# One store in twenty is cut into 119 and 9 partitions

## The chip, the cores and the metric

The kernel runs on one core of one Trainium2 chip. The metric is the device time of one execution in microseconds. The core has five engines that run their own instruction streams: TensorE (PE), VectorE (DVE), ScalarE (ACT), GpSimd (POOL) and SyncE (SP). SP computes nothing here; it issues DMAs, which sixteen DMA engines carry out.

## The reference

It is the forward and the backward pass of decode attention: one query row for each of 2 x 32 heads, against 8192 keys and values of width 128, all in bf16.

```python
B, H, Sq, Sk, D = 2, 32, 1, 8192, 128

def _fwd_reference(q, k, v):
    scale = q.shape[-1] ** -0.5
    scores = jnp.einsum("bhqd,bhkd->bhqk", q, k) * scale
    p = _softmax(scores, axis=-1)
    return jnp.einsum("bhqk,bhkd->bhqd", p, v)

def reference(q, k, v, grad_out):
    _out, _vjp = jax.vjp(_fwd_reference, q, k, v)
    _grads = _vjp(grad_out)
    return (_out, *_grads)
```

K and V of a head are 2 MB each. So 64 heads read 268 MB, and the gradients dK and dV write as much again. The output and dQ are small.

## The kernel before, in words

A head's K and V are loaded whole, as tiles `kt` and `vt` of 128 partitions x 64 rows x 128 (`load`, L103). Partition p holds 64 consecutive rows, which are 16 KB of contiguous memory. Five such pairs exist (`UNITS = 5`).

TensorE transposes the rows eight at a time against an identity (`transposes`, L112). ScalarE, and for two steps in sixteen VectorE, copies the transposes out of PSUM (L119, L117), and TensorE multiplies them with the query and with the output's gradient (`products`, L135). Softmax and its gradient then need a few small operations per head (L159 to L227). The weighted sums for the output and dQ are matmuls over the untransposed rows (`weighted_rows`, L240).

dV and dK are outer products of a weight per row with one row of `grad_out` or `q`. VectorE writes them into the buffers from which the rows came (`outer`, L270): dV into `vt`, and dK into `kt`, four pieces of 16 rows each. After the fourth piece `store` (L278) writes the whole 2 MB tile to memory; w = 0 is dV and w = 1 is dK. For the last head alone it stores halves of 1 MB.

The order is written out by hand (`manual_schedule`). In iteration h the program works on head h (transposes, products, softmax) and finishes head p = h - 1 (weights, outer products, stores). At its end it issues the load of head h + 3 into the pair of buffers that head h - 2 has left:

```python
if j == 7:
    if x and UNITS <= h + 3 < BH:
        load(h + 3)
```

All loads and stores of K, V, dK and dV are issued by SP in this order, so in the middle of the run each iteration gives SP a dV store, a dK store, a K load and a V load. A load waits until the store out of its buffer has landed. What stands behind a waiting DMA in SP's order waits with it. The two small inputs and the two small outputs go through ACT's DMA queue.

Of the kernel before, what the change touches and what calls it, by code (L numbers as in the profile page):

```python
# [15 lines left out]
HC = CH // 2  # L16
QG = 4
OG = 4
UNITS = 5


@with_exitstack
def kernel(
# [11 lines left out]
    nc = tc.nc  # L35
    B, H, Sq, D = q.shape
    Sk = k.shape[2]
    P = nc.NUM_PARTITIONS
# [3 lines left out]
    assert NT * P == Sk and NT == 4 * CH and BH <= P and BH % QG == 0  # L42
    assert BH % OG == 0 and OG * 8 == 32
    NS = 2 * NT // CH
# [9 lines left out]

    pick = const.tile([P, 4, 2, OG], F32)
    idv = ident_f[:].rearrange("p (g w k j) -> p g j w k", g=4, w=2, k=OG)
    nc.vector.tensor_copy(out=pick[:], in_=idv[:, 0])
    for g in range(1, 4):
# [6 lines left out]

    kvp = ctx.enter_context(tc.tile_pool(name="kv", bufs=UNITS))
    evp = ctx.enter_context(tc.tile_pool(name="ev", bufs=5))
# [8 lines left out]
    dk_v = out_2.rearrange("b h (p n) d -> (b h) p n d", n=NT)  # L76
    dv_v = out_3.rearrange("b h (p n) d -> (b h) p n d", n=NT)
# [8 lines left out]
    wz = [  # L86
        [const.tile([P, NT // 4, 32], BF16, name=f"wz{w}{k}") for k in range(OG)]
        for w in range(2)
# [5 lines left out]
    heads = [Head() for _ in range(BH)]  # L94

    def load(h):
        x = heads[h]
        x.kv = [
            kvp.tile([P, NT, D], BF16, name="kt", tag="kt"),
            kvp.tile([P, NT, D], BF16, name="vt", tag="vt"),  # L100
        ]
        for dst, src in zip(x.kv, (k_v, v_v)):
            nc.sync.dma_start(out=dst[:], in_=src[h])  # L103
# [79 lines left out]
    def to_weights(h, w, src):  # L183
        k = h % OG
        nc.vector.tensor_copy(  # L185
            out=wz[w][k][:, :, 16 * w + 4 * k : 16 * w + 4 * k + 4],
            in_=src[:].rearrange("p (m j) -> p m j", j=4),
        )
# [44 lines left out]
    def weighted_rows(h, w, chunks):  # L233


        rows, k = heads[h].kv[1 - w], h % OG
        for c in chunks:
# [37 lines left out]
        )  # L275

    def store(h, w, a=0, b=NT):
        nc.sync.dma_start(out=(dv_v, dk_v)[w][h][:, a:b, :], in_=heads[h].kv[1 - w][:, a:b, :])  # L278

    def outer_and_store(h, w, i):  # L280

        outer(h, w, i)
        if h == BH - 1:
            if i % 2:
                store(h, w, (i - 1) * CH, (i + 1) * CH)
        elif i == NT // CH - 1:
            store(h, w)
# [13 lines left out]
    with tc.manual_schedule():  # L301
        for h in range(min(UNITS, BH)):
            load(h)
        for h in range(BH + 1):
# [4 lines left out]
            for j in range(NS):  # L309
# [31 lines left out]
# [3 lines that stand above are left out]
# [38 lines left out]
```

## Time and profile before

| what | value |
|---|---|
| three runs | 1332.49, 1332.11, 1324.77 us; median 1332.11 |
| the profiled execution, its own time | 1328.14 us |
| its span, first to last instruction | 1326.3 us |
| PE, ACT, DVE busy | 84%, 68%, 67% of the span |
| DMA queue of SP | 536.89 MB, 98.2% of sixteen engines' span |
| data read and written, over the span | 405 GB/s |
| K loads and V loads, issue to landing (median) | 25.4 us, 30.2 us |
| dV stores and dK stores, issue to landing (median) | 34.8 us, 39.5 us |

The DMA share is the mean over the sixteen engines of the time in which a packet was under way. A packet here is one partition's 16 KB. Issue to landing counts from SP's instruction until all parts of the transfer have arrived, time in the DMA engines' own queues included. The profile does not number the DMA engines. It does keep, for each DMA, the times of the sixteen steps by which its semaphore rises.

### The profile page before, as it was taken

How to read it: one execution, taken by the hardware profiler on the slowest of the kernel's cores; microseconds unless marked ns; L12 is line 12 of the kernel's file. 1: busy time of each engine (PE TensorE's matmuls, PEld its weight loads, DVE VectorE, ACT ScalarE, POOL GpSimd, SP SyncE). 2: the span in 40 equal slices, each digit the busy share in tenths (PEclk: the TensorE clock that was granted, in tenths of full speed). 3: DMA queues.
4: the chain of work that ended last, by engine and by line, in shares of the span. 5: the costliest groups of instructions: out<-in, count | busy, mean ns of one | idle time of the engine just before them, and what ended most of it. 6: DMA issues, size and time to landing. Idle time of an engine off the chain costs nothing.

```text
span 1326.3 us, 42070 instructions
## 1 busy us (share of the span) xinstructions
PE 1108.8 (84%) x18948; PEld 909.2 (69%) x18948; DVE 887.3 (67%) x1511; ACT 906.7 (68%) x1043; POOL 4.8 (0%) x16
## 2 busy tenths in 40 slices
PE   5999898898788887888879878798888888898883
PEld 5777777776676766766767667676766676676762
DVE  2887777676666766767657666575766666676664
ACT  5877787776766766767677676676766676676662
POOL 1000000000000000000000000000000000000000
PEclk9999999988988989989799888987988888888886
DMA  9999999999999999999999999999999999999985
GB/s 396 422 427 426 428 426 428 427 427 429 426 426 419 421 413 417 419 412 415 412 410 405 406 403 400 405 405 401 400 397 409 395 406 403 397 401 392 410 371 242
DMA packets 37652, 539.64 MB, mean 407 GB/s; under 512 B 4448, under 2 KB 4448, under 8 KB 4448
## 3 DMA queue, kind: packets, MB, share of 16 engines
q1 hardware_dynamic: 37152, 536.89, 98.2%
q8 instruction: 148, 2.42, 0.6%
q14 instruction: 32, 0.26, 0.0%
q10 hardware_dynamic: 320, 0.07, 0.0%
HBM read 268.47 MB, written 268.47 MB: 405 GB/s over the span
## 4 chain that ended last, share of the span: by engine, by line
DMA 63%; PE 21%; ACT 8%; DVE 4%; issue 1%; SPq 1%; ACTq 0%; DVEq 0%
DMA out_dram<-kt 36%; DMA kt<-in_k_dram 27%; PE tp L112 13%; ACT ev L119 8%; PE acc L240 5%; DVE ev L117 3%; PE sm L135 2%; DMA nat<-in_grad_out_dram 1%; PE dp L205 1%; DVE kt L270 1%; PE dp L135 1%; SPq L103 0%; SPq L278 0%; PE sm L169 0%; DVE vt L270 0%
## 5 line engine op out<-in xcount | busy, mean ns | idle before, releaser
L119 ACT CAST ev<-tp 128x1024 bf16<-128x1024 f32 x896 | 879.2, 1026 | 379.3 <-PE tp L112 364.4
L112 PE MATMUL tp<-ident_bf,kt 128*128 128x128 bf16 x4096 | 379.9, 247 | 119.2 <-DMA kt<-in_k_dram 115.1
L112 PEld LDWEIGHTS <-kt 128*128 128x128 bf16 x4096 | 280.2, 110 | 256.0 <-issue 133.8
L117 DVE CAST ev<-tp 128x1024 bf16<-128x1024 f32 x128 | 156.7, 1224 | 298.5 <-PE tp L112 293.5
L112 PE MATMUL tp<-ident_bf,vt 128*128 128x128 bf16 x4096 | 313.4, 219 | 48.2 <-ACT ev L119 38.0
L135 PEld LDWEIGHTS <-ev 128*128 128x128 bf16 x8192 | 333.0, 100 | 2.2 <-issue 0.2
L112 PEld LDWEIGHTS <-vt 128*128 128x128 bf16 x4096 | 259.1, 98 | 81.6 <-issue 73.1
L270 DVE TENSOR_TENSOR kt<-qd,dS 128x2048 bf16<-128x2048 bf16 x256 | 310.0, 1212 | 0.0
L270 DVE TENSOR_TENSOR vt<-qd,P 128x2048 bf16<-128x2048 bf16 x256 | 295.8, 1217 | 0.0
L135 PE MATMUL dp<-doT_all,ev 128*128 128x1 bf16 x4096 | 180.3, 165 | 0.1
L135 PE MATMUL sm<-qT_all,ev 128*128 128x1 bf16 x4096 | 178.0, 164 | 0.0
L240 PE MATMUL acc<-vt,wz 128*32 128x512 bf16 x1024 | 127.8, 489 | 4.7 <-DVE wz L185 4.5
L240 PE MATMUL acc<-kt,wz 128*32 128x512 bf16 x1024 | 106.1, 407 | 0.5 <-DVE wz L185 0.5
L240 PEld LDWEIGHTS <-wz 128*32 128x32 bf16 x2048 | 53.7, 95 | 16.3 <-DVE wz L185 6.8
L159 DVE TENSOR_REDUCE mp<-sm 128x1 f32<-128x64 f32 x64 | 14.4, 225 | 55.1 <-PE sm L135 55.1
L205 PE MATMUL dp<-ld,ones_f 128*128 128x2 f32 x128 | 27.8, 287 | 10.4 <-DVE ld L192 9.5
L205 PEld LDWEIGHTS dp<-ld,ones_f 128*128 128x128 f32 x128 | 23.3, 228 | 17.8 <-DVE ld L192 17.5
L210 DVE RECIPROCAL rl_all<-dp 128x1 f32<-128x1 f32 x64 | 10.7, 168 | 34.7 <-PE dp L205 34.7
L153 ACT CAST qd<-pb 128x1024 bf16<-128x1024 f32 x16 | 16.2, 1012 | 12.3 <-PE pb L145 12.3
L169 PE MATMUL sm<-gm,ones_f 1*128 1x1 f32 x128 | 24.2, 256 | 0.0
L169 PEld LDWEIGHTS sm<-gm,ones_f 1*128 1x128 f32 x128 | 18.7, 182 | 6.6
L174 ACT ACTIVATE E_f<-sm,negm 128x64 f32<-128x64 f32 x64 | 23.1, 361 | 0.0
(40 smaller groups left out, 263.2 us busy)
## 6 DMA issues: line engine op xcount, KB each, us to landing
kt<-in_k_dram SPq DMA_DIRECT2D x64, 2048.0 KB, 25.4
vt<-in_v_dram SPq DMA_DIRECT2D x64, 2048.0 KB, 30.2
out_dram<-vt SPq DMA_DIRECT2D x63, 2048.0 KB, 34.8
out_dram<-kt SPq DMA_DIRECT2D x63, 2048.0 KB, 39.5
out_dram<-vt SPq DMA_DIRECT2D x2, 1024.0 KB, 12.0
out_dram<-kt SPq DMA_DIRECT2D x2, 1024.0 KB, 12.1
out_dram<-rows ACTq DMA_DIRECT2D x2, 16.0 KB, 5.8
nat<-in_q_dram ACTq DMA_DIRECT2D x1, 16.0 KB, 8.1
```

Of the source, the lines that this page charges most:

```text
L112: nc.tensor.matmul(tp[:, i, :], lhsT=x.kv[w][:, n, :], rhs=ident_bf[:], start=True, stop=True)
L117: nc.vector.tensor_copy(out=ev[:], in_=tp[:])
L119: nc.scalar.copy(out=ev[:], in_=tp[:])
L135: nc.tensor.matmul((x.dp if w else x.sm)[:, n : n + 1], lhsT=ev[:, i, :], rhs=col, start=True, stop=True,)
L153: nc.scalar.copy(out=qd[:], in_=pb[:])
L159: nc.vector.reduce_max(out=x.mp[:], in_=x.sm[:, 0:NT], axis=AX.X)
L169: nc.tensor.matmul(mb, lhsT=ones_f[0:1, :], rhs=x.gm[:], start=True, stop=True)
L174: nc.scalar.activation(out=x.E[:], in_=x.sm[:, 0:NT], func=ACT.Exp, bias=negm[:], scale=scale, accum_out=x.ld[:, 0:1],)
L205: nc.tensor.matmul(x.lsum, lhsT=ones_f[:], rhs=x.ld[:], start=True, stop=True)
L210: nc.vector.reciprocal(out=rl, in_=x.lsum[:, 0:1])
L240: nc.tensor.matmul(acc[32 * g : 32 * g + 32, :], lhsT=wz[w][k][:, n // 4, :], rhs=rows[:, n : n + 4, :].rearrange("p n d -> p (n d)"), sta ...
L270: nc.vector.tensor_tensor(out=x.kv[1 - w][:, n : n + CH, :].rearrange("p n (d t) -> p n d t", t=2), in0=row.unsqueeze(1).to_broadcast([P, ...
```

## The change

A store whose number 2h + w leaves 10 when divided by 20 is issued as two DMAs, one for partitions 0 to 118 and one for partitions 119 to 127. The first runs on the first seven DMA engines with 17 partitions on each, the second on the first nine with one on each. All other stores are issued as before, as one DMA over 128 partitions on sixteen engines. The bytes and the order of SP are otherwise the same.

```diff
+FEW = 119
+RARE = 20
 UNITS = 5
...
     def store(h, w, a=0, b=NT):
-        nc.sync.dma_start(out=(dv_v, dk_v)[w][h][:, a:b, :], in_=heads[h].kv[1 - w][:, a:b, :])
+
+        cuts = (0, FEW, P) if (2 * h + w) % RARE == RARE // 2 else (0, P)
+        for lo, hi in zip(cuts, cuts[1:]):
+            nc.sync.dma_start(
+                out=(dv_v, dk_v)[w][h][lo:hi, a:b, :], in_=heads[h].kv[1 - w][lo:hi, a:b, :]
+            )
```

## The prediction

> **What bounds the kernel now.** I began with the page's slices and queues. One queue moves everything and keeps the engines 98% busy, yet its rate falls from 427 to about 400 GB/s, and in the last slice to 242.
>
> ```profile
> DMA  9999999999999999999999999999999999999985
> GB/s 396 422 427 426 428 426 428 427 427 429 426 426 419 421 413 417 419 412 415 412 410 405 406 403 400 405 405 401 400 397 409 395 406 403 397 401 392 410 371 242
> ...
> q1 hardware_dynamic: 37152, 536.89, 98.2%
> ```
>
> Next the waits of the issuing queue (SP's own). It spends most of the span waiting to issue a load (L103) until an earlier dK store (`out_dram<-kt`) has landed, so the loads follow the landing of stores; PE, ACT and DVE, 67 to 84% busy, follow the loads.
>
> ```profile
> SPq L103 <- DMA out_dram<-kt: 943.2, 55, 19.5
> SPq L278 <- DVE vt L270: 136.9, 14, 22.1
> SPq L278 <- DVE kt L270: 88.0, 32, 7.2
> ```
>
> Which landing is waited for shows at the end of the run, in the view of stretches (the last two figures are DMA share and GB/s) and in the issues of the last 18 us:
>
> ```profile
> 100.00:380.00 280.00, 245.82 (x4405) 201.79 (x4403) 205.36 (x351) 210.09 (x241) 0.00 (x0) 0.95 1.01 427
> 860.00:1100.00 240.00, 206.13 (x3401) 168.62 (x3401) 157.58 (x272) 161.12 (x185) 0.00 (x0) 0.84 1.00 401
> 1318.00:1326.00 8.00, 0.00 (x0) 0.00 (x0) 0.00 (x0) 0.00 (x0) 0.00 (x0) 0.50 0.05 23
> ...
> out_dram<-kt SPq DMA_DIRECT2D x2, 1024.0 KB, 12.1
> ```
>
> A share of 0.05 is about one engine of sixteen (1/16 is 0.06), at 23 GB/s: for the last 7 us one engine alone still works off a backlog. The records behind these views tell the same of the whole run. Each DMA raises its semaphore in sixteen steps, one for each engine's part. I took the time between the last steps of successive 2 MB DMAs, and between their first steps:
>
> - 130 to 380 us: last step, loads 4.86 us, stores 5.37 us apart; first step, 4.86 and 4.87.
> - 860 to 1100 us: last step, loads 5.14, stores 5.35; first step, 5.59 and 4.90.
>
> So one engine needs 5.37 us for its eight 16 KB packets of a store (0.671 us each), the quick ones 4.87 (0.609); loads cost all the same at first. From the first store on the packet records show one unbroken chain of about 0.67 us packets during stores, and only one. Its lag behind the quickest grows by 0.51 us a store: 4.65 us at 139 us, 15.95 us at 360 us (22 stores between). Near 18.5 us it stops growing: four DMAs, some 20 us, are all that SP has outstanding when it waits, so the quick engines run dry and the slow one sets the pace. 128 stores times 0.5 us is 64 us of the span.
>
> **The change, part by part.** *Where.* The condition holds for 2h+w = 10, 30, 50, 70, 90, 110: six dV stores (heads 5, 15, 25, 35, 45, 55), none at the end. The changed program's SP order has six more DMAs, nothing else differs on any engine.
>
> *Issue.* Six more issues of 0.43 to 0.47 us on SP (the mean row of a store in mid-run). The dK store and the next pair of loads stand behind them. SP waits up to 19.5 us per group at L103, so this costs nothing; without that cover it would be 6 x 0.45 = 2.7 us. The rotation of completion semaphores shifts, but an issue then waits at most for the DMA eight places back, older than the store whose landing its buffer needs anyway. The second part adds no wait of its own. The next load into that buffer waits for both parts; the store's slow half is its part on the seven engines, priced below.
>
> *Rows.* A plain store gives each engine 8 packets. Split, engines 0 to 6 get 17 + 1 = 18, engines 7 and 8 get 1, engines 9 to 15 none. Over six stores: +60, -42 and -48 packets.
>
> *If the slow engine is one of 9 to 15* it loses 48 x 0.671 = 32.2 us. It is never idle, so all of this leaves the end: 1326.3 - 32.2 = 1294.1 us of span (42 x 0.671 = 28.2 us, so 1298.1, if it is 7 or 8).
>
> *Engines 0 to 6 are then nearly as loaded.* The quick stretch of 100 to 380 us is their pace: 536.87 MB of loads and stores at 427 GB/s are 1257.3 us, instruction fetches included. That is an upper value, because the slow engine is in the mean; by the quick engines' own 4.862 us a DMA it would be 256 x 4.862 = 1244.7. Added 60 x 0.609 = 36.5 us, 1.8 us before the first packet and 1.0 us between the last landing and the end: 1296.6 us by the upper pace, 1284.0 by the lower. I take the upper, since it was measured over 280 us with everything running. The later of the two ends is 1296.6, and they are within 3 us of each other: this many splits about evens the two out.
>
> *Does skew stall the queue?* Each split puts engines 0 to 6 back by 10 x 0.609 = 6.1 us and the slow one forward by 5.4, in all 11.5 us; between two splits the slow one loses 20 x 0.5 = 10 us. The lag swings by about 11 us, under the 18.5 us at which engines run dry. Cost nil; engines 9 to 15 bar the slow one run ahead and idle, which is free.
>
> *Packets on seven engines.* The trace holds no such store. Lower bound: the plain 0.609 us. Upper bound: around 50 us, at the first turn from loads to stores, packets on most engines took about 1.0 us; 108 packets (6 x 18) with 0.39 us more are 42 us. I take the plain packet, as the nearest in kind and size.
>
> *Late slowness.* After 620 us the slow engine's loads grow to 5.14 us. If engines 0 to 6 suffer that too, it is 0.28 us for some 61 loads, 17 us; if the lag never locks the others into one rhythm, nothing. I take nothing for the sum and keep 17 us for the range.
>
> *The sum.* 1296.6 + (1328.14 - 1326.3) = 1298.4 us against the profiled execution's 1328.1, or 2.2% less. The median of the runs shown is 1332.1, 4 us above the profiled one, so beside it this is 2.5%.
>
> *Two rules of the skill.* The row first: only one engine is late, and the queues let it be 18.5 us late. The Trainium skill, "DMA: Bandwidth & Descriptors", Rules for kernel authors, says to use all sixteen engines and so speaks against a store confined to seven; if a store's own duration were on the path, 17 packets instead of 8 would add 9 x 0.609 x 6 = 33 us and give 1361. Row two: the records do not number the engines. The same page, Latency and other measured facts, calls engines 7 and 15 usually slower than the rest; by it the slow one is relieved (1294 to 1298 for its own end), by no row here is its number shown.
>
> **The rivals.**
>
> *1. The slow engine is one of 0 to 6.* Then it gets 60 more packets at 0.671 = 40.3 us: 1328.1 + 40.3 = 1368.4, slower by 3%. The trace speaks neither for nor against, as the semaphore steps of a DMA are alike; it decides from the first split on, since that engine is never idle. By count of engines alone this has 7 of 16.
>
> *2. The gain is spent on engines 0 to 6.* The move is right, but seven engines reading 119 partitions at once, or the late slowness, delay them. With 17 us of late slowness and 0.062 us more on each of 108 packets (a slow engine's packet), 6.7 us: 1298.4 + 23.7 = 1322. For it: the slowing of loads after 620 us. Against: no such slowing before 380 us, when engines were out of step as they will be again.
>
> *3. The split store gates SP.* If the dK landing that SP awaits came 6.1 us later each time with nothing left in the quick engines' queues, 6 x 6.1 = 36.5 us, so 1364.7. Against: SP has four DMAs, 20 us, outstanding.
>
> *4. The split does not land on seven and nine engines* (say both parts go to one engine). 127 or more packets on one engine, 77 us a time, would pass the 18.5 us of slack by 59 us, six times: over 1650 us. The program shows 119 and 9 rows as the change says; I give this 0.01.
>
> **How the numbers follow.** Blind counting gives 9 of 16 for relief and 7 of 16 against; I put relief at 0.83, well above the count, and this step is a judgement that no row supplies. Of the 0.83, 0.76 is for the forecast and 0.07 for rival 2. Rivals 1, 3 and 4 share the other 0.17: 0.14, 0.02, 0.01. This kernel's runs scatter by 0.6%, so about 1% can be told from no change: below 1318.8 is faster (0.76), to 1345 the same (0.07), above slower (0.17). The forecast is the likeliest case, 1298.4. Its own range goes from the lower pace, 1284.0 + 1.8 = 1286, to 1317; the whole range must hold 0.8 and so takes in rival 2 as well: 1285 to 1327.
>
> **What would show it.** In the changed kernel's profile the rate should stay near 415 to 425 GB/s past 400 us instead of falling to 400; SP's wait on `out_dram<-kt` should remain long; the last 8 us should no longer be one engine's alone, or by less; the 119-partition store should land 6 us or more later after its issue than a plain one near it, six times. Rival 1 would show a rate falling below 400 and a longer lone tail; rival 2 a rate of 405 with an even end. If the lone tail is unchanged and the time with it, my reading of one slow engine as the limit is wrong.

## Result and profile after

The changed kernel is slower. Its median is 1410.75 us (1409.02 to 1412.35, four runs) beside 1330.23 us (1324.77 to 1332.49, four runs) for the kernel before: a ratio of 1.061, with a 95% interval of 1.057 to 1.065. That is 80.5 us, or 13.4 us for each of the six cut stores. The profiled execution took 1409.02 us with a span of 1407.2 us.

The page's slices and queue of the changed kernel:

```profile
DMA  9999999999899999989999989999989999988995
GB/s 399 419 428 427 404 419 421 412 417 386 311 387 402 398 402 405 350 326 395 393 406 400 358 321 391 393 394 409 367 321 385 397 403 403 390 341 348 398 370 243
...
q1 hardware_dynamic: 37152, 536.89, 94.7%
```

The bytes and packets are those of before. The rate has six dents, one for each cut store: a small one (404) in the fifth slice, where little lag had built up, and five deep ones, to between 311 and 341. A slice is 35 us. Between the dents it is about 400, as before, so the pace between cuts was not relieved either.

The waits of the issuing queue (SP's own), and the issues with their median time to landing:

```profile
SPq L105 <- DMA out_dram<-kt: 1026.9, 56, 26.5
SPq L283 <- DVE vt L272: 112.8, 11, 21.3
SPq L283 <- DVE kt L272: 58.4, 22, 6.7
...
out_dram<-kt SPq DMA_DIRECT2D x63, 2048.0 KB, 40.6
out_dram<-vt SPq DMA_DIRECT2D x57, 2048.0 KB, 36.0
out_dram<-vt SPq DMA_DIRECT2D x6, 1904.0 KB
...
out_dram<-vt SPq DMA_DIRECT2D x6, 144.0 KB
```

SP still waits for the landing of dK stores, 84 us longer in all, and the waits for VectorE's dV and dK became shorter. The bound is the one of before, only later: the added time is DMA time. The view of stretches says the same (the last two figures are DMA share and GB/s). 345 to 352 and 373 to 379 us lie in the second cut:

```profile
860.00:1100.00 240.00, 191.80 (x3238) 157.36 (x3237) 150.31 (x251) 154.82 (x178) 0.00 (x0) 0.86 0.96 381
345.00:352.00 7.00, 5.93 (x121) 5.39 (x118) 4.92 (x8) 6.81 (x10) 0.00 (x0) 1.00 0.63 257
373.00:379.00 6.00, 2.30 (x52) 2.08 (x49) 2.46 (x4) 2.79 (x5) 0.00 (x0) 0.97 0.47 195
1399.00:1407.00 8.00, 0.00 (x0) 0.00 (x0) 0.00 (x0) 0.00 (x0) 0.00 (x0) 0.50 0.05 22
```

A share of 0.47 means that only seven or eight of sixteen engines have a packet under way; the others wait for SP. The last 8 us are one engine's alone, exactly as before.

The landing steps of each DMA (sixteen for a whole store, seven and nine for the two parts) show one cut from inside. The second cut was issued at 330.2 us:

```
DMA                         quick engines landed         slow engine landed
V load before it            341.9 to 344.2 (two: 351)    361.10
119 partitions, 7 steps     352.7 353.8 354.3 357.0 361.4 362.0     377.51
9 partitions, last step                                  378.17
dK store after it                                        383.07
```

The part on seven engines does contain the slow one. It needed 377.51 - 361.10 = 16.4 us for 17 packets, 0.97 us each, where its plain store costs 5.37 us (0.67 each). In the six cuts the figure was 13.9, 16.4, 15.3, 15.0, 15.1 and 14.5 us: 15.0 in the mean, 0.88 us a packet.

From one dK landing to the next (one head) the kernel before takes 20.2 to 21.4 us. Here the six cut heads take 29.6, 31.9, 31.0, 31.1, 31.2 and 30.4 us. Against the same heads before, that is +61.4 us. The twelve heads beside them add 10.7 us, all others together 8.5.

### The profile page after: what moved, and what is told of

Same layout as the page of the kernel before. It is cut to its first block, busy times and chain, and to the rows that moved or that the text cites. A ratio compares the mean times of both kernels' runs of the same rounds, so it can differ in the third digit from the quotient of the medians.

```text
span 1407.2 us, 42082 instructions
## 1 busy us (share of the span) xinstructions
PE 1115.2 (79%) x18948; PEld 915.6 (65%) x18948; DVE 887.3 (63%) x1511; ACT 906.6 (64%) x1043; POOL 4.8 (0%) x16
## 4 chain that ended last, share of the span: by engine, by line
DMA 67%; PE 20%; ACT 7%; DVE 3%; issue 1%; SPq 0%; ACTq 0%; DVEq 0%
DMA out_dram<-kt 37%; DMA kt<-in_k_dram 30%; PE tp L114 12%; ACT ev L121 7%; PE acc L242 4%; DVE ev L119 2%; PE sm L137 2%; DMA nat<-in_grad_out_dram 1%; PE dp L137 1%; PE dp L207 1%; DVE kt L272 1%; DVE vt L272 0%; PE c L260 0%; PE sm L171 0%; SPq L105 0%
## 5 line engine op out<-in xcount | busy, mean ns | idle before, releaser
L114 PE MATMUL tp<-ident_bf,kt 128*128 128x128 bf16 x4096 | 387.5, 250 | 195.5 <-DMA kt<-in_k_dram 191.2
L114 PEld LDWEIGHTS <-kt 128*128 128x128 bf16 x4096 | 286.2, 112 | 334.3 <-DMA kt<-in_k_dram 199.3
L212 DVE RECIPROCAL rl_all<-dp 128x1 f32<-128x1 f32 x64 | 10.7, 168 | 35.6 <-PE dp L207 35.6
```

What stands on the lines that cost most here:

```text
L114: nc.tensor.matmul(tp[:, i, :], lhsT=x.kv[w][:, n, :], rhs=ident_bf[:], start=True, stop=True)
L212: nc.vector.reciprocal(out=rl, in_=x.lsum[:, 0:1])
```

## The experiments

Two things had to be told apart: which engine is slow, and what a packet of a cut store costs. Each experiment differs from the kernel before only as its diff shows, unless said otherwise. Times "of before" are of the same chip.

### Which engine is the slow one

**Pieces of growing size.** The six stores that the change cuts are cut into 1, 2, 3, 4, 5, 6, 7 and 100 partitions, which go to 1, 2, 3, 4, 5, 6, 7 and 10 engines.

```diff
+        cuts = (0, 1, 3, 6, 10, 15, 21, 28, P) if (2 * h + w) % 20 == 10 else (0, P)
+        for lo, hi in zip(cuts, cuts[1:]):
+            nc.sync.dma_start(
+                out=(dv_v, dk_v)[w][h][lo:hi, a:b, :], in_=heads[h].kv[1 - w][lo:hi, a:b, :]
+            )
```

> The six stores that the change cuts into 119 + 9 are cut here into 1, 2, 3, 4, 5, 6, 7 and 100 partitions, which divide over 1, 2, 3, 4, 5, 6, 7 and 10 engines. Theory A (rival 1 of the prediction: the slow engine is one of the first seven): in mid-run one engine is some 18 us behind, so from some size on every one of these DMAs has one step of its semaphore 10 us or more after the others, and no smaller one has; the size at which it begins is the number of the slow engine, counted from one. Theory B (the slow engine is not among the first seven, and the cut store itself stalls something): the pieces of 1 to 7 have no such late step.

At the cut of 752 us the landing steps, counted from each piece's issue, were:

```
piece of      all steps but the last      last step
1 to 4        none, up to 17.8, 14.9, 10.7  17.6, 18.0, 15.1, 10.9
5             up to  6.2                       15.8
6             up to  3.4                       11.1
7             up to  3.0                        6.9
```

From the piece of five partitions on, one step comes long after the others; pieces of one to four have no such step. The cuts at 964 and 1176 us show the same. So the slow engine is the fifth, and the 119-partition part holds it: rival 1's condition. That a DMA on k engines takes the lowest-numbered k is stated by the Trainium skill, "DMA: Bandwidth & Descriptors", How many engines (k); the steps here agree with such a nesting. The run took 1358.63 us (before 1326.69).

**A store on five engines.** Three dV stores are cut into 115 (23 packets on each of five engines) and 13.

```diff
+        cuts = (0, 115, P) if 2 * h + w in (24, 56, 88) else (0, P)
```

> The three dV stores that were cut into 124 + 4 partitions on four engines (23 us slower than before) are cut into 115 + 13: 23 packets on each of five engines and one on each of thirteen, so 24 on the first five instead of 32 on the first four. If the fifth engine is the slow one, it gets 16 packets more three times and pays 0.9 us or so for each of the 24: 3 x (24 x 0.9 - 5.4) = 49 us, with some 2 us around each cut 1380 us or more. If it is not, the smaller pieces cost less than those of 124 + 4: 1340 to 1348 us.

1389.22 us, ratio 1.046 (1.045 to 1.048): 20 us a cut. The four-engine cut below gives its engines more packets (32 against 24) and cost 7 us a cut. The two also differ in the partitions that each engine gets, but the landing steps point to the fifth: here one engine lands 14 to 18 us after all others between the cuts (from 450 us on), there the last engine is 2 to 7 us behind the one before it.

### What a cut costs apart from that

**Equal shares.** The same six stores as 112 + 16 partitions: 7 + 1 packets on every engine, as in a plain store.

```diff
+        cuts = (0, 112, P) if (2 * h + w) % 20 == 10 else (0, P)
```

> The same six stores are cut into 112 + 16 partitions, 7 + 1 on each of sixteen engines, so that the cut and its extra issue stay but no engine gets more than before. Theory A (extra packets on the slow engine): no difference, within 0.5% of the kernel before. Theory B (a store in two DMAs, or the shifted rotation of semaphores, stalls): most of the 80 us return, 1380 to 1410 us.

1357.21 us, ratio 1.023 (1.021 to 1.026). Neither theory gave this: no engine carries more, and yet each cut costs 5 us. The slow engine's cut store took 6.5 us at the first cut and 5.2 to 7.1 later, against 5.37, which is 6 us in all. More is lost just before it: from the second cut on, the slow engine's two plain stores ahead of the cut one, which it works off while the others, up to 20 us ahead, are in the cut, take 12.2 to 14.3 us together instead of 10.7. So plain stores of one engine take longer while others work off the cut.

**Halves.** Every store as two DMAs of 64 partitions, 4 packets per engine each.

```diff
+        cuts = (0, 64, P)
```

> Every store goes as two DMAs of 64 partitions, four packets on each engine in both. Theory E (the slowness belongs to the engine): one engine still needs 5.37 us for the eight packets of a store pair, and the time stays within 1% of before. Theory P (it belongs to the eight partitions that this engine otherwise serves): they are now spread over two engines, each of which loses half, 0.25 us a store, so the time falls by about 30 us, 2.3%.

1363.21 us, ratio 1.027 (1.023 to 1.032). The lag of one engine is gone (the last landing is 0 to 6 us after the one before it, where the kernel before goes up to 17), and the kernel is slower all the same. The spread over all engines is near 10 us until 370 us and some 18 from 450 us on, as wide as before. So cutting costs something of its own, and I needed it without the slow engine.

**Transfers alone.** Loads and stores in the same order, without the computation; the buffers are stored as loaded. The diff shows the added lines; the lines of the computation, which go, are left out, here and in the runs built on this one.

```diff
+            if h:
+                for w in range(2):
+                    if p == BH - 1:
+                        store(p, w, 0, NT // 2)
+                        store(p, w, NT // 2, NT)
+                    else:
+                        store(p, w)
+                if UNITS <= h + 3 < BH:
+                    load(h + 3)
```

> All loads and stores of K, V, dK and dV in the same order through the same buffers, with no computation between (the outputs hold the inputs). Theory X (one DMA engine is slow in stores by itself): last steps of successive stores are still 5.37 us apart against 4.87 for the quick engines, and the time is about 128 x 4.86 + 128 x 5.37 = 1309 us and a few for start and end. Theory Y (the slowness comes from what the compute engines do): all sixteen engines need 4.87, and the time is about 256 x 4.87 = 1247 us and a few.

1254.27 us. Loads and stores land 4.8 to 5.0 us apart on the quickest engine and on the last, and the spread of landings stays under 3.5 us: the slow engine is not slow by itself.

**Transfers with one engine's work.** To these, first 8192 TensorE matmuls against the identity (64 heads x 128), then instead ScalarE copies and VectorE products.

```diff
+                for c in range(16):
+                    tp = ps_tp.tile([P, HC, P], F32, name="tp", tag="tp")
+                    for i in range(HC):
+                        n = (c % 8) * HC + i
+                        nc.tensor.matmul(
+                            tp[:, i, :], lhsT=heads[h].kv[c // 8][:, n, :], rhs=ident_bf[:],
+                            start=True, stop=True,
+                        )
```

> The run without computation, in which all sixteen engines kept 4.87 us a store, with TensorE's 8192 transposes of K and V put back, their results left in PSUM (the outputs hold the inputs). Theory T (the slow stores come with TensorE's stream of instructions): one engine is again late, its stores some 5.4 us apart, and the time goes from 1254 to about 1310 us. Theory V (they come with VectorE or ScalarE): all engines keep 4.87 and the time stays near 1255.

```diff
+                for c in range(16):
+                    ev = evp.tile([P, HC, P], BF16, name="ev", tag="ev")
+                    nc.scalar.copy(out=ev[:], in_=heads[h].kv[c // 8][:, (c % 8) * HC : (c % 8 + 1) * HC, :])
...
+                    for i in range(4):
+                        t = heads[p].kv[1 - w]
+                        nc.vector.tensor_tensor(
+                            out=t[:, i * CH : (i + 1) * CH, :], in0=t[:, i * CH : (i + 1) * CH, :],
+                            in1=t[:, i * CH : (i + 1) * CH, :], op=ALU.mult,
+                        )
```

> The run without computation with sixteen copies of 128 x 1024 on ScalarE and eight products of 128 x 2048 on VectorE put back for each head, nothing on TensorE (dV and dK hold squares of the inputs, the small outputs hold inputs). Theory T: all engines keep 4.87 us a store, 1255 us and some waiting. Theory V: one engine is late, stores near 5.4 us apart, about 1310 us.

With TensorE 1275.41 us: one engine lags again, about 0.17 us a store in the mean where the whole kernel has 0.51, and the spread reaches 17 us. With ScalarE and VectorE 1256.18 us; no engine lags like that (the last lands at most 0.9 us after the one before it). The slow engine thus comes with TensorE's work. This run holds 43% of the kernel's TensorE instructions and shows a third of the lag, and the view of stretches shows why. It is cut at the last landing steps of one head: V load, dV store, dK store, next K load (first figure the length, second the time in which TensorE is busy):

```profile
474.27:479.12 4.85, 4.81 (x46) 4.81 (x47) 0.00 (x0) 0.00 (x0) 0.50 1.01 432
479.12:484.39 5.27, 5.10 (x85) 4.93 (x83) 0.00 (x0) 0.00 (x0) 0.94 1.00 426
484.39:489.28 4.89, 0.00 (x0) 0.00 (x0) 0.00 (x0) 0.00 (x0) 0.73 1.00 426
489.28:494.10 4.82, 0.00 (x0) 0.00 (x0) 0.00 (x0) 0.00 (x0) 0.50 1.02 435
```

From 200 to 1100 us the late engine's dV stores take 5.27 us, with TensorE busy in 87% of that time, and its dK stores 4.86, with TensorE idle; loads take 4.84 and 4.86, though TensorE is busy in 99% of the V load. In the whole kernel TensorE is busy in 99% and 92% of this engine's dV and dK stores, and both take 5.37. So the engine is slow in stores that run beside TensorE's work, one of two here and both in the whole kernel. Instruction fetches (queue q8) come with TensorE too, 148 packets in the kernel before, 64 here and none in the other two runs, but they are not the reason: a fetch delays its engine by some 1.4 us at once, and the late engine's chain of packets of 0.66 us runs on unbroken beside it (for one, at 272.7 us of the kernel before).

**The change without a slow engine.** Transfers alone, with the change's own cut.

```diff
+        cuts = (0, 119, P) if (2 * h + w) % 20 == 10 else (0, P)
```

> The run without computation with the six stores cut into 119 + 9 partitions. No engine is slow here, so only the extra packets of engines 0 to 6 are left. Theory L (a plain packet, 0.609 us): these engines get 60 packets more, 36.5 us, 1254 + 37 = 1291 us, and each part of 17 lands some 10.4 us after the part before it. Theory C (partitions read away from their usual engine collide with other stores, 0.9 to 1.0 us a packet): 17 packets take 15 us or more and the time is near 1320 us.

1362.31 us against 1254.27 for transfers alone: +108 us, more than the change costs in the whole kernel. The page's slices and queue of this run:

```profile
GB/s 397 427 432 431 395 426 429 431 428 412 299 407 406 422 429 431 345 348 394 420 421 425 364 335 408 408 418 423 388 328 402 396 414 424 413 325 360 395 413 218
...
q1 hardware_dynamic: 37152, 536.89, 95.9%
```

The same six dents, with no slow engine and no computation. At the first cut all engines were in step: they landed the load before it at 139.6 to 140.6 us, and the seven parts at 151.2, 151.3, 151.3, 152.5, 154.0, 155.5 and 156.9: 11 to 16 us for 17 packets, about 0.67 to 0.96 us each.

**The same cut in dK stores,** behind which come loads instead of a store.

```diff
+        cuts = (0, 119, P) if (2 * h + w) % 20 == 11 else (0, P)
```

> As the run without computation with six cut stores, but the dK stores after those are cut (2h+w = 11, 31, ..., 111), so that loads and no other store follow the cut one on the free engines. Theory C (a packet of the cut store is slow while other engines store): at the first cut, where the engines are in step, the 17 packets take about 10.4 us on every one of the seven engines, against 11.4 to 16.4 us when a dV store was cut; later cuts, at which engines 0 to 6 are some 17 us behind and the others are storing again, cost about 12 us each, so the time stays above 1320 us. Theory M (seven engines that read 119 partitions are slow by themselves): the first cut takes 11 to 16 us here too.

1355.74 us. The first cut again took 11 to 18 us (landings 155.6 to 164.0 after 144.5 to 147.6). Until 154.3 us the other engines had only loads and the small second part; then the next dV store began on them. Packets of up to 1.6 us instead of 0.61 begin at 146 us, so other engines' plain stores are not needed for the cost; the cut's own engines must be in each other's way, or the loads must.

**Halves without computation.** Transfers alone, every store as two of 64 partitions.

```diff
+        cuts = (0, 64, P)
```

> The run without computation with every store as two DMAs of 64 partitions, four packets on each engine in both, so that all engines have the same bytes but read other partitions than with one DMA. Theory C: the first stores, with the engines in step, take well over 4.87 us (3 to 4.5 us a half), and the time is 2% or more above 1254. If equal shares are free wherever the partitions lie, a half takes 2.44 us and the time stays within 1% of 1254.

1310.88 us, 4.5% more than transfers alone, with equal shares on all engines. The first halves took 2.4 to 4.3 us, where 4 packets of 0.609 are 2.4.

**The cause: which partitions are read together.** In transfers alone, the stores of the last heads, behind which no load stands, are issued as 16 DMAs of 8 partitions each.

```diff
+        steps = {(61, 1): (1, 1), (62, 0): (4, 4), (62, 1): (1, 4), (63, 0): (4, 1), (63, 1): (2, 2)}
...
+        for i in range(16):
+            cut = [slice(i // s * 8 * s + i % s, i // s * 8 * s + i % s + 7 * s + 1, s) for s in steps[h, w]]
+            nc.sync.dma_start(out=dst[cut[1], :, :], in_=src[cut[0], :, :])
```

> Loads and stores alone, no computation, so dV and dK hold V and K themselves, and some rows land in another order. The last three heads' stores, behind which no load stands, are each issued as 16 DMAs of 8 partitions: 16 packets of 16 KB on each of eight engines, 2 MB in all, five times with other partitions and other rows of memory in one DMA. Names: S1 means that one DMA reads 8 neighbouring partitions, S2 every second, S4 every fourth; D1, D2, D4 the same for the places of memory that it writes. Every packet, its size, the number of DMAs and the engines are the same in all five; the time is read from the landing steps of each store's 16 DMAs. Theory S (groups of four neighbouring partitions hang on one path, which carries one 16 KB packet in 0.607 us whoever asks for it; 1214 ns packets are two engines on one path): S1 has four engines on each of two paths, so 16 x 4 x 0.607 = 38.9 us for S1D1 and for S1D4; S2D2 two engines on each of four, 19.4 us; S4D4 and S4D1 one engine on each of eight, 9.7 us. Theory D (the shared path is on the side of the memory): S1D1 and S4D1 38.9 us, S4D4 and S1D4 9.7 us. Theory F (it is slow to use few engines, or DMAs of a few packets, whatever they read): all five alike, between 9.7 us and some 15 us. The Trainium skill, SBUF — State Buffer, section Door 1: The DMA port swizzle, speaks for theory S: its map puts partitions 0 to 3 on one port and gives 27 GB/s a port as the asymptote, an estimate of 38.6 us for 2 MB over two ports.

The view of stretches of this run, one stretch inside each of the five stores, in the order S1D1, S4D4, S1D4, S4D1, S2D2 (the last two figures again DMA share and GB/s):

```profile
1229.00:1240.00 11.00, 0.00 (x0) 0.00 (x0) 0.00 (x0) 0.00 (x0) 1.00 0.45 122
1241.00:1250.00 9.00, 0.00 (x0) 0.00 (x0) 0.00 (x0) 0.00 (x0) 1.00 0.48 195
1253.00:1271.00 18.00, 0.00 (x0) 0.00 (x0) 0.00 (x0) 0.00 (x0) 1.00 0.45 101
1273.00:1281.00 8.00, 0.00 (x0) 0.00 (x0) 0.00 (x0) 0.00 (x0) 1.00 0.46 191
1284.00:1297.00 13.00, 0.00 (x0) 0.00 (x0) 0.00 (x0) 0.00 (x0) 1.00 0.49 140
```

The share is the same throughout, 7.2 to 7.8 of sixteen engines busy, but the rate is not: equally busy engines carry 191 to 195 GB/s when a DMA reads every fourth partition, 140 when every second, and 101 to 122 when neighbours. What is done with the rows of memory makes no such difference (S4D1 is as fast as S4D4, S1D4 no faster than S1D1). The packet records give the mean packet: 619 and 630 ns for S4, 907 ns for S2, 952 and 1164 ns for S1. So theories D and F fall. Theory S holds in its order, not in its size: the slowest store took 21 us where 38.9 were expected. The landing steps show why not: the eight engines do not stay in step but drift over several of the 16 DMAs, and so onto different groups of partitions.

The Trainium skill, "SBUF — State Buffer", Door 1: The DMA port swizzle, maps four neighbouring partitions, and those 32 further on, to one of 16 ports. This run agrees as to neighbours at steps 1, 2 and 4; the distance of 32 was not varied alone.

### Could the idea pay if the work goes to the right engines?

**Four engines.** Three dV stores as 124 + 4: 32 packets on engines 0 to 3, none on the fifth.

```diff
+        cuts = (0, 124, P) if 2 * h + w in (24, 56, 88) else (0, P)
```

> Three dV stores (heads 12, 28, 44) are cut into 124 + 4 partitions, which divide over four engines, 31 + 1 packets each; engines 4 to 15 get none. If the slow engine is the fifth, it loses 3 x 8 x 0.671 = 16 us, engines 0 to 3 get 72 packets or 44 us more, which their slack of some 60 us covers: about 1311 us, 1.2% faster. If it were one of the first four, it would get 72 packets and the time would rise by 48 us or more. If the cut stores cost more than their packets, as the even cut did (30 us for six), the gain goes: 1320 to 1330.

1348.98 us, ratio 1.018 (1.012 to 1.023). Between the cuts the pace is better: from the second to the third a head takes 19.4 to 20.4 us instead of 20.6 to 21.2. The view of stretches shows it, 860 to 940 us, first of before, then of this kernel:

```profile
860.00:940.00 80.00, 71.38 (x1153) 58.16 (x1154) 53.44 (x92) 54.57 (x63) 0.00 (x0) 0.81 1.00 403
```

```profile
860.00:940.00 80.00, 70.16 (x1206) 57.55 (x1202) 56.26 (x95) 57.84 (x68) 0.00 (x0) 0.89 1.01 427
```

But the three cut heads take 42.3, 40.9 and 40.5 us, 62 us more than before, which is more than the gain of some 39 us outside them. Nor is that gain the 24 packets taken from the slow engine, 16 us. After a cut four engines are late together (of the K load issued at 662.5 us, twelve engines' parts landed by 670.2 and four at 679.0 to 688.0), and the last steps of stores are 4.87 us apart: the engines that the cut put back set the pace, with plain packets, and the slow one is no longer the latest.

**Part of the rows.** Every fifth store sends rows 0 to 55 of each partition as before, and the last eight as 124 + 4.

```diff
+        if b - a == NT and (2 * h + w) % 5 == 2:
+            parts = [(0, P, 0, 56), (0, 124, 56, NT), (124, P, 56, NT)]
```

> In every fifth store (25 of them) the last 8 of 64 rows per partition go as 124 + 4 partitions on four engines, the first 56 as one DMA on sixteen: the fifth engine loses one packet's worth of eight, 25 x 0.67 = 17 us in all, and engines 0 to 3 get three packets' worth more, 25 x 1.8 = 46 us, inside their slack of some 60. With such small pieces collisions should be few: about 1312 us, 1.2% faster. If every store cut off its usual partitions costs several us, as the even cut did, it is slower than before: 1350 us or more.

1355.11 us, ratio 1.022 (1.019 to 1.026). The smaller skew did not help: from the second on, each cut head takes 21.4 to 23.8 us, the heads between them 19.3 to 21.1.

**Four engines that start apart.** Four dV stores as 92 + 36.

```diff
+        cuts = (0, 92, P) if 2 * h + w in (24, 48, 72, 96) else (0, P)
```

> Four dV stores (heads 12, 24, 36, 48) are cut into 92 and 36 partitions: 23 packets on each of engines 0 to 3, which start 23 partitions apart and so never read the same group of four neighbours at the same time as one another (in 124 = 4 x 31 they start 31 apart, 32 being one round of the groups, and mostly do), and 3 on each of engines 0 to 11. The fifth engine has 5 packets fewer four times: 20 x 0.671 = 13.4 us. Theory A (the cost is the cut's own engines meeting on one path): packets at 0.61 us, the slow engine keeps the pace: 1315 us, 1% faster than before. Theory B (they also meet the engines whose paths these are, which are busy with the neighbouring loads and stores all the time): packets at 0.9 to 1.16 us as in S2D2 and S1D4; engines 0 to 3 then have 1257 + 4 x (18 x 0.61 + 26 x 0.3 to 0.55) = 1332 to 1358 us and set the time: no gain. The Trainium skill, SBUF — State Buffer, section Door 1: The DMA port swizzle, puts two partitions that differ by 32 on one port, which is where the 32 comes from; no run here has varied that distance alone.

1338.84 us, ratio 1.009 (1.006 to 1.012): slower than before by 0.9%, at theory B's lower end. The first cut head took only 24.3 us, the later three 34.7 to 35.5. In the second and third cut the last landing came 20.4 and 18.9 us after the one before the cut; if that is one engine's, its 26 packets took 0.73 to 0.78 us each: cheaper than the 0.9 to 1.16 of theory B, dearer than 0.61. Theory A falls. That the rest comes from meeting the engines to which these paths belong was not shown by itself, and no run shows which partitions of a cut store each engine takes; the expectation counts them in consecutive runs. No version beat the kernel before.

## Why the prediction was wrong, point by point

- **What bounds the kernel: right.** One engine sets the pace, in stores and, from 620 us on, in V loads, and SP has about 18.5 us of slack. (The 5.14 us that the prediction read for late loads is a mean: K loads stay at 4.84, V loads take 5.44.) Without computation, where no engine lags, the transfers take 1254 us, near the 1244.7 us plus ends that the quick engines' pace gave. When, after a four-engine cut, the slow engine is no longer the latest, the rate between cuts returns to 427 GB/s.
- **Where the parts land, and the issues: right.** Seven and nine landing steps. SP's added issues are hidden: its long wait only grew.
- **The slow engine's number: wrong, and by the prediction's own sums this turns the sign.** The step that failed is "relief at 0.83". Nine of sixteen engines was all that counting gave, and no row gave more. The engine is the fifth, so it was loaded with ten packets per cut and not relieved of eight. The Trainium skill, "DMA: Bandwidth & Descriptors", Latency and other measured facts, calls engines 7 and 15 usually slower and guesses at a cause in DMAs issued from GpSimd, of which this kernel has none; the pieces and the five-engine store measure the fifth.
- **"Packets on seven engines": the term was mis-sized, in rival 1 too.** The plain 0.609 us was taken (0.671 for the slow engine). In the changed kernel the slow engine's packets took 0.88 us in the mean, and without computation the seven engines' took 0.67 to 0.96. The stated upper bound, about 1.0 us, held; the choice of the low end did not. The argument "nearest in kind and size" left out that a whole store reads its partitions in another arrangement: the run with every first, second and fourth partition shows that this can set the packet's time. That it does so in the cut of 119 is inferred from that run and from the cuts with equal shares; no run varied the arrangement inside this cut. Rival 2 had the mechanism, seven engines reading 119 partitions at once, at 6.7 us; without computation the cut cost 108 us where its plain packets are 36.5. Rival 1 gave 1368.4 us for this reason and not 1409: of the 80 us, 40 are the ten packets at 0.671, and 17 x (0.88 - 0.67) x 6 = 21 us this term.
- **"Does skew stall the queue? Nil": wrong.** With the slow engine in the split, both go the same way: the others run ahead, the spread of landings goes from 18 to 20 us up to 36, and they run dry. That lies beside the slow engine's own time and costs nothing there. What remains of the 80 us, 19 us, lies in the heads around. About 15 us of it is the slow engine's V loads (343 us in all, 328 before), which take 5.5 to 5.6 us from the second cut on, where before they take 4.9 until 580 us and some 5.3 to 5.45 after 620 us. This is the "late slowness" that was put at nothing; it starts earlier here. Why V loads alone is not known.
- **Even with the guess right, a gain was unlikely.** With no slow engine and no computation, the same cut cost 108 us over transfers alone, 18 us a cut, and those 1362 us are already more than the whole kernel before takes (1330); the relief would have been 32 us in all. The case itself, a slow engine outside the seven, was not run.
- **The tests named beforehand:** the rate fell below 400 GB/s (381 at 860 to 1100 us), as rival 1 said. The lone tail did not grow, which rival 1 had said it would: the lag is capped by SP's slack, so the tail is the same for any slow engine. It was no test. The 119-partition parts did land later after their issue than plain dV stores (46 to 47 us from the second cut on, where the median of plain ones is 36.0), but both readings let one expect that.

## What to carry to other kernels

A DMA over fewer or other partitions is not a plain one with other shares: price its packets from a run of it with nothing else in the program, before counting what it relieves. An engine whose number no row shows is worth one run of small pieces on 1, 2, 3 ... engines, since the sign of such a change hangs on it; a judgement does not replace it. When one engine paces a queue, a higher rate between the edits need not mean that it was relieved: engines that the edit put back may have become the latest. Read which engines land last, and the bill for the edits in the heads where they stand.

## What the runs showed of the hardware

- The fifth engine's stores take 5.37 us for 2 MB beside 4.86 of the others, only with TensorE at work: none of it without computation (1254.27 us) or with ScalarE and VectorE (1256.18 us). In the run with 43% of TensorE's instructions one engine's stores take 5.27 us while TensorE works and 4.86 while it rests. Why that engine, and how TensorE slows it, stays open.
- On eight engines the same 16 KB packets take 0.62 us when a DMA reads every fourth partition, and 0.95 to 1.16 us when it reads neighbours; the arrangement in memory made no such difference (195 and 191 GB/s, 122 and 101).
- A store as two halves of 64 partitions, each on all sixteen engines, made a program of transfers alone 4.5% longer.
